# Cosine attention and FNet block on one core: new step priorities, other filler matmuls, and batch 1's scaling on two engines

## The chip, the cores and the metric

The kernel runs on one core of a Trainium2 chip. The metric is the device time of one launch in microseconds, as the median of three runs. The engines are TensorE (PE, matmuls), VectorE (DVE), ScalarE (ACT), GpSimd (POOL) and SyncE (SP, which here only issues DMAs). Each engine runs its own instructions in the order in which they were written; they meet through semaphores.

## The reference

```python
# q, k, v: (8, 12, 448, 64); w_ch1: (768, 3072); w_ch2: (3072, 768)
q_n = q / (np.linalg.norm(q, axis=-1, keepdims=True) + 1e-06)
k_n = k / (np.linalg.norm(k, axis=-1, keepdims=True) + 1e-06)
scores = np.matmul(q_n, k_n.transpose(0, 1, 3, 2)) / tau
attn = softmax(scores)
x = np.matmul(attn, v)            # heads side by side: (8, 448, 768)
u = x + np.real(np.fft.fft(np.fft.fft(x, axis=1), axis=2))
un = (u - mean(u)) / np.sqrt(var(u) + 1e-06)
out = u + np.maximum(un @ w_ch1, 0.0) @ w_ch2
```

## The kernel before

Eight batches go through four stages each: the norms and scaling of Q and K, attention, the two-dimensional Fourier mix, and a feed-forward block (FFN) with its layer norm. The stages of neighbouring batches overlap: while the FFN of batch b fills TensorE, the norms and the attention of batch b+1 run beside it.

**The order is planned when the kernel is built.** `Plan.add` (line 109) takes each step with the engines that may run it, an estimated length for each of them, a priority (`prio`, smaller goes first), the names that it reads and writes and, for a DMA, a time that the transfer takes on the queues (`serve`). `Plan.schedule` (line 153) then places step after step on the engine on which it can start earliest, breaking ties by priority; ScalarE and VectorE may wait a little for a more urgent step. A DMA is taken to land `DMA_LAT` (2.0 us) after its issue plus its `serve` time, shared with the other queue (lines 268 to 273). The result is one fixed list for each engine; `Plan.emit` (line 307) writes it out, with a semaphore wait for each dependency. At run time nothing is reordered: a step that waits holds everything behind it on its engine.

**Priorities** are 10 + 100 x batch for the norms, 13 to 18 above that for attention, 30 for the Fourier mix, and 5000 for the matmuls of the FFN, so that attention goes ahead of them. `SHIFT` (line 29) adds a number to single steps by name: `"t40": {0: 278.9}` makes the step t40 less urgent by 278.9.

**GpSimd and VectorE.** `PIECE` (line 58) and `PORT` (line 59) describe to the planner that GpSimd's elementwise steps are cut into pieces, and that certain VectorE steps that fall into such a piece are held until its end.

**Norms.** Batches 0 and 1 go through `first_norm` (line 577): the loads of K, Q and the tails in two groups of six heads (line 620), squares on ScalarE (627), sums on VectorE (631), `norms` (566; lines 571 to 575: logarithm, exponential, a small addition, a reciprocal), then the scaling: for each group three K, three Q steps of 128x384 (line 657) and three tail steps of 128x128 (line 653), all on VectorE. TensorE transposes the scaled tiles by matmuls with an identity (steps tk, tq, tt; lines 681, 693 to 695 and 706), and ScalarE or VectorE copies them out of PSUM (672, 716). The loads of batch 1 are put into the place of W2's chunks 5 to 11, which are loaded over them afterwards (line 553, on GpSimd's DMA queue). Batches 2 to 7 go through `norm` (line 719): GpSimd scales in pieces of 128x256 (line 764) and a DMA on SP's queue transposes (line 770).

**Attention** (`attn`, line 775): scores by row-paired matmuls (843, 855, 856), exponentials on ScalarE (823), the product with V (874, 880), and the division on VectorE (898, 900). **Fourier mix** (`fold`, 908, and `fft`, 984): folds on VectorE, two matmul stages (962 or 967, and 1005), sums into U (1021, 1033). The layer norm (1062 to 1071) writes UN; for batches 1 to 7 a DMA on SP's queue transposes it into UNT (line 1092).

**FFN.** `up` (1122): six matmuls a hidden tile against W1 (line 1137), then a ReLU out of PSUM (1153). `prod` (1161): the second matmuls (1168). Batches 1 to 7 pair their row tiles and save one product of eight by the Strassen-Winograd sums: of the hidden tiles on VectorE (`comb`, line 1263), and once of W2 (`sums`, line 1308: steps t1k to t4k for k = 0 to 2; t1 and t2 go before t4 by their operands; VectorE at line 1324 or GpSimd in four pieces at line 1326).

**Fillers.** `Plan.fill` (line 284) goes through TensorE's planned list and puts filler matmuls, whose results nobody reads, into planned gaps if a PSUM bank is free then. One filler step is 11 matmuls of 62 columns, planned at 0.34 us, one for each 0.4 us of the gap. It waits for the VectorE step that is the last planned to have ended by then. The first call (line 1381) covers 7.5 us to the first matmul of the FFN and fills gaps over 0.3 us; the second (line 1382) covers the rest and fills gaps over 1.2 us.

Of the kernel before, what the change touches and what calls it, by code (L numbers as in the profile page):

```python
# [26 lines left out]
DMA_LAT = 2.0  # L27

SHIFT = {
# [28 lines left out]
PIECE = {r"sc\d_\d": 0.63, r"f[avm]\dp_\d": 0.54, r"t\d\d": 0.94}  # L58
# [39 lines left out]
class Plan:  # L98
# [54 lines left out]
    def schedule(self):  # L153
# [65 lines left out]
        while left:  # L219
# [48 lines left out]
            if op.dma is not None:  # L268
                if t > now:
                    flow["sp"], flow["pool"] = drain(now, t)  # L270
                    now = t
                flow[e].append([op, op.end + DMA_LAT, op.serve])
                drain(now, None)
                if e == "sp":
                    sync.append(op)
# [8 lines left out]
    def fill(self, t0, t1, after, make, least=0.3):  # L284

        live = {x: [] for x in (0, 1, 2, 4, 6)}
        for op in self.ops:
            for t in op.acquire or ():
                live[t.slot if t.pool == "M" else 2 + 2 * t.slot].append((op.start, max(u.end for u in t.users), t))
# [1148 lines left out]
```

## Time and profile before

| what | before |
|---|---|
| median of 3 runs (lowest, highest) | 595.78 us (595.0, 596.48) |
| profiled execution | 595.06 us |
| its span, first to last instruction | 593.2 us |
| granted TensorE clock, mean | 0.996 |
| TensorE busy | 573.8 us (97%) |
| VectorE busy | 424.1 us (71%) |
| ScalarE busy | 352.0 us (59%) |
| GpSimd busy | 234.1 us (39%) |
| fillers (line 1377), TensorE | 418 matmuls before the FFN, 121 behind |

The first line of the profile's second part cuts the span into 40 slices of 14.8 us and gives busy tenths (9 is 90% or more); the lines below it give the clock that TensorE was granted and the DMA engines' share:

```profile
PE   5899899999899999999999999999999999999997
DVE  6979788888788868876888678976776469512222
POOL 8844235659554255523360454413540210200302
PEclk9999899999999999999999999999999999999999
DMA  9999997954289249584494179543931010310101
```

A busy TensorE here is one that has a matmul in its pipeline, not one at its peak, and the ends of matmuls are modelled. The groups of the scaling and of the DMA transposes, as the profile lists them (line, engine, operation, what it writes and reads, shape, count, busy us and mean ns; for DMAs the size and the time from issue to landing):

```profile
L764 POOL TENSOR_TENSOR QH<-STG,SM 128x256 bf16<-128x256 f32 x126 | 80.9, 668 | 83.1 <-DVE SM L575 65.9
UNT<-F SPq DMA_TRANSPOSE x25, 2.8
QT<-QH SPq DMA_TRANSPOSE x24, 4.1
KT<-QH SPq DMA_TRANSPOSE x18, 2.9
```

### The profile page before, as it was taken

How to read it: one execution, taken by the hardware profiler on the slowest of the kernel's cores; microseconds unless marked ns; L12 is line 12 of the kernel's file. 1: busy time of each engine (PE TensorE's matmuls, PEld its weight loads, DVE VectorE, ACT ScalarE, POOL GpSimd, SP SyncE). 2: the span in 40 equal slices, each digit the busy share in tenths (PEclk: the TensorE clock that was granted, in tenths of full speed). 3: DMA queues.
4: the chain of work that ended last, by engine and by line, in shares of the span. 5: the costliest groups of instructions: out<-in, count | busy, mean ns of one | idle time of the engine just before them, and what ended most of it. 6: DMA issues, size and time to landing. Idle time of an engine off the chain costs nothing.

```text
span 593.2 us, 15707 instructions
## 1 busy us (share of the span) xinstructions
PE 573.8 (97%) x6477; PEld 446.8 (75%) x6477; DVE 424.1 (71%) x975; ACT 352.0 (59%) x674; POOL 234.1 (39%) x344
## 2 busy tenths in 40 slices
PE   5899899999899999999999999999999999999997
PEld 4679687687578688778778688678878788778684
DVE  6979788888788868876888678976776469512222
ACT  7895787347865886458657756368537644224140
POOL 8844235659554255523360454413540210200302
PEclk9999899999999999999999999999999999999999
DMA  9999997954289249584494179543931010310101
GB/s 215 128 218 218 173 183 141 164 131 102 64 155 144 27 126 128 121 143 101 75 169 85 41 161 112 137 82 81 139 83 30 15 54 1 94 38 5 53 1 55
DMA packets 187640, 62.17 MB, mean 105 GB/s; under 512 B 166704, under 2 KB 185392, under 8 KB 187568
## 3 DMA queue, kind: packets, MB, share of 16 engines
q1 hardware_dynamic: 129648, 38.35, 34.3%
q0 software_dynamic: 57920, 22.81, 30.5%
q8 instruction: 51, 0.84, 0.6%
q14 instruction: 21, 0.17, 0.1%
HBM read 51.90 MB, written 11.01 MB: 106 GB/s over the span
## 4 chain that ended last, share of the span: by engine, by line
PE 84%; POOL 6%; DMA 4%; DVE 3%; SPq 2%; issue 1%; ACT 1%; POOLq 0%; DVEq 0%; ACTq 0%
PE PS L1137 34%; PE PS L1168 33%; PE PS L880 5%; PE PS L843 5%; DMA W2b<-in_k_dram 3%; SPq L620 2%; PE PS L967 2%; PE PS L874 2%; PE PS L1005 2%; POOL TX L1326 1%; DMA W1b<-in_moe_w_ch_dram 1%; PE PS L855 1%; POOL W1b L552 1%; POOL U L478 1%; PE PS L856 1%
## 5 line engine op out<-in xcount | busy, mean ns | idle before, releaser
L1137 PE MATMUL PS<-UNT,W1b 128*128 128x256 bf16 (+1 forms) x2304 | 236.3, 260 | 0.5 <-DVE HQ L1153 0.3
L1137 PEld LDWEIGHTS PS<-UNT,W1b 128*128 128x128 bf16 x2304 | 198.7, 98 | 25.4 <-issue 3.7
L823 ACT ACTIVATE E<-PS 128x900 bf16<-128x900 f32 x192 | 147.8, 827 | 31.8 <-PE PS L843 30.4
L1168 PE MATMUL PS<-W2b,HQ 128*128 128x384 bf16 x768 | 133.5, 326 | 0.0
L1153 ACT ACTIVATE HQ<-PS 128x512 bf16<-128x512 f32 x117 | 69.8, 598 | 87.7 <-PE PS L1137 86.7
L764 POOL TENSOR_TENSOR QH<-STG,SM 128x256 bf16<-128x256 f32 x126 | 80.9, 668 | 83.1 <-DVE SM L575 65.9
L1168 PEld LDWEIGHTS PS<-W2b,HQ 128*128 128x128 bf16 x768 | 73.5, 98 | 45.7 <-issue 1.7
L1263 DVE TENSOR_TENSOR HQ<-HQ 128x512 bf16<-128x512 bf16 x141 | 67.9, 502 | 44.2 <-ACT HQ L1153 31.1
L1193 POOL TENSOR_TENSOR OUTB<-OUTB,U 128x192 f32<-128x192 f32 x66 | 38.8, 608 | 139.2 <-ACT OUTB L1188 138.6
L1168 PE MATMUL PS<-TX,HQ 128*128 128x384 bf16 x396 | 69.9, 326 | 0.0
L1168 PEld LDWEIGHTS PS<-TX,HQ 128*128 128x128 bf16 x396 | 38.2, 98 | 24.2 <-issue 0.7
L880 PE MATMUL PS<-VB,E 128*128 128x65 bf16 x1152 | 51.1, 193 | 0.0
L757 DVE TENSOR_REDUCE SM<-QH 128x6 f32<-128x384 f32 x84 | 44.2, 536 | 8.5 <-ACT QH L755 8.2
L880 PEld LDWEIGHTS PS<-VB,E 128*128 128x128 bf16 x1152 | 47.6, 97 | 1.2
L1153 DVE TENSOR_SCALAR HQ<-PS 128x512 bf16<-128x512 f32 x45 | 31.1, 690 | 23.4 <-PE PS L1137 22.3
L755 ACT ACTIVATE QH<-STG 128x384 f32<-128x384 f32 x84 | 42.7, 521 | 6.2 <-DVE SM L757 6.0
L1222 POOL DMA_INDIRECT out_dram<-OUTB,IDX x20 | 20.8, 1039 | 63.9 <-DVE OUTB L1200 50.0
L843 PE MATMUL PS<-QT,KT 64*128 64x225 bf16 x576 | 39.9, 260 | 2.6 <-DVE X L900 2.3
L874 PE MATMUL PS<-VZ,E 128*128 128x130 bf16 x192 | 41.6, 219 | 0.5 <-ACT E L823 0.4
L1033 DVE TENSOR_TENSOR U<-ACG,X 128x384 bf16<-128x384 f32 (+3 forms) x70 | 39.8, 590 | 0.8
L1188 ACT ACTIVATE OUTB<-PS 128x384 f32<-128x384 f32 x33 | 16.2, 491 | 37.0 <-PE PS L1168 36.9
L843 PEld LDWEIGHTS PS<-QT,KT 64*128 64x128 bf16 x576 | 22.6, 94 | 16.3 <-issue 4.9
(134 smaller groups left out, 659.7 us busy)
## 6 DMA issues: line engine op xcount, KB each, us to landing
STG<-in_q_dram SPq DMA_DIRECT2D x18, 384.0 KB, 3.9
STG<-in_k_dram SPq DMA_DIRECT2D x18, 384.0 KB, 3.8
VB<-in_v_dram POOLq DMA_DIRECT2D x24, 192.0 KB, 6.9
W1b<-in_moe_w_ch_dram POOLq DMA_DIRECT2D x12, 384.0 KB, 6.4
W2b<-in_moe_w_ch_dram POOLq DMA_DIRECT2D x12, 384.0 KB, 6.9
out_dram<-OUTB SPq DMA_DIRECT2D x7, 384.0 KB
TX<-in_q_dram SPq DMA_DIRECT2D x2, 576.0 KB, 6.3
TX<-in_k_dram SPq DMA_DIRECT2D x2, 576.0 KB, 6.6
```

Of the source, the lines that this page charges most:

```text
L755: P.add("act", lambda a, sq=sq, src=buf[:, w * x:w * x + w]: a.activation(sq, src, ACTF.Square), t_act(w), pr, f"sq{i}_{b}", reads=bn, wri ...
L757: P.add("dve", lambda v, o=SS[:, i, H // ns * x:H // ns * (x + 1)], sq=sq: v.tensor_reduce(o, sq.rearrange("p (h d) -> p h d", d=DH), AX.X ...
L764: r = v.tensor_tensor(v3(qh)[:, h:h + 4], v3(buf)[:, h:h + 4], RN[:, i, h:h + 4].unsqueeze(2).to_broadcast((128, 4, DH)), AluOp.mult)
L823: return a.activation(o, self.PS[:, bk:bk + nc_, 0:SQ2], ACTF.Exp, scale=1.0 / self.tau)
L843: i = pe.matmul(self.PS[:, bk + h, c0:c0 + NK], self.KT[r, jj, kt * 128:(kt + 1) * 128], self.QT[r, jj, cols], start=True, stop=True)
L874: r = pe.matmul(o, st(6), self.VZ[:, j, :], start=not split, stop=(split and i == 0), skip_group_check=True)
L880: r = pe.matmul(o[:, 65 * h:65 * h + 65], st(2 * kt + h), self.VB[:, kt, 2 * j + h, :], start=(split and i == h == kt == 0), stop=((not sp ...
L1033: return v.tensor_tensor(U[o0:o0 + n, ut, cs].rearrange("p (i e) -> p i e", e=2), src, X[i0:i0 + n, x, cs].rearrange("p (i e) -> p i e", e ...
L1137: r = pe.matmul(self.PS[:, bk, x * n:(x + 1) * n], self.W1b[:, j, ft * 128:(ft + 1) * 128], self.UNT[:, j, cs], start=(j == 0), stop=(j == ...
L1153: return e.activation(o, i, ACTF.Relu) if e is self.nc.scalar else e.tensor_relu(o, i)
L1168: r = pe.matmul(self.PS[:, bk, 0:n], lhs(f), rhs(f), start=(start and f == 0), stop=(stop and f == NF // 2 - 1), skip_group_check=True)
L1263: P.add("dve", lambda v: v.tensor_tensor(cs(o), cs(a), cs(bq), op), 0.46, -0.5, f"{nm}{k}_{b}", reads=rd, writes=hr(o)(k))
```

## The change

Five things are changed, and the rest of the kernel is as before.

1. The scaling steps of batch 1 may go to VectorE or GpSimd, whichever the planner finds; GpSimd is planned at 0.98 us for K and Q and 0.42 us for a tail, as one piece each. Batch 0 stays on VectorE.
2. The planner takes a DMA transpose to land 0.4 us (`TR_LAT`) instead of 2.0 us after its issue, plus 1.3 us of `serve`, where it had 1.75 us for Q and K and 1.0 us for the normalized tiles.
3. A filler step is 6 matmuls of 128 columns instead of 11 of 62.
4. Fillers go into planned gaps from 0.4 us. Behind the start of the FFN they do so only where TensorE's planned use in some window of 3.4 us around the gap is under 0.75; the transposes tk, tq and tt count half in it. The last 20 us of the plan get none.
5. The table `SHIFT` is new throughout, so that the order of steps on every engine, the issues of DMAs among them, can differ.

The diff, with most of the table left out:

```diff
--- before.py
+++ after.py
@@ -25,37 +25,38 @@
 SEM_LAT = 0.11
 PE_LAT = 0.2
 DMA_LAT = 2.0
+TR_LAT = 0.4
 
 SHIFT = {
-    "ktd0": {0: 17.1}, "ix0": {0: -3.7}, "ix3": {0: 215.9}, "vz1": {0: 14.4}, "pads": {0: 1.8}, "ld_q0_0": {0: -131.9}, "ln0": {1: 4.8},
...
-    "pv21_1": {0: 2.3}, "x3_1": {0: -177.5}, "f10_1": {0: 97.4}, "ex5_1": {0: -284.8}, "relu16_0": {0: 127.8}, "t40": {0: 278.9}, "t32": {0:
...
+    "ix1": {0: 80.5}, "ld_k0_0": {0: -4.9}, "ldt0": {0: 60.6}, "nrm0": {0: -132.9, 2: -29.4, 3: 2.5}, "sqT0_0": {0: 86.3}, "scT2_0": {0: -6.6},
...
+    48.9}, "sqQ0_1": {0: -78.5}, "ln1": {1: 1.2}, "scK0_1": {0: 171.1}, "scK2_1": {0: 36.4}, "ek1_1": {0: -432.7}, "tq1_1": {0: 14.3},
+    "ld_t1_1": {0: -353.2}, "sqK1_1": {0: -6.1}, "ssK1_1": {0: 257.7}, "sqQ1_1": {0: -56.6}, "sqT1_1": {0: -2.4}, "tq4_1": {0: -139.8}, "tq5_1":
...
+    "t10": {0: -141}, "t40": {0: 441.4}, "t42": {0: 425.9}, "pq0_1": {1: 139.9}, "u0_1": {1: -96.4}, "pq1_1": {0: -32.8}, "u1_1": {0: 0.3, 5:
...
 }
 
 
 
-PIECE = {r"sc\d_\d": 0.63, r"f[avm]\dp_\d": 0.54, r"t\d\d": 0.94}
+PIECE = {r"sc[KQ]\d_1": 0.98, r"scT\d_1": 0.42, r"sc\d_\d": 0.63, r"f[avm]\dp_\d": 0.54, r"t\d\d": 0.94}
 PORT = r"eps\d|f[a01]\d_\d|g\d_\d|u\d+_\d|un\d_\d|s\d\d_\d|t\d\d|sc[KQT]\d_\d"
 
 
@@ -269,7 +270,7 @@
                 if t > now:
                     flow["sp"], flow["pool"] = drain(now, t)
                     now = t
-                flow[e].append([op, op.end + DMA_LAT, op.serve])
+                flow[e].append([op, op.end + (TR_LAT if op.name[:2] == "tr" else DMA_LAT), op.serve])
                 drain(now, None)
                 if e == "sp":
                     sync.append(op)
@@ -281,20 +282,24 @@
                     put(n)
         return max(op.end for op in self.ops)
 
-    def fill(self, t0, t1, after, make, least=0.3):
+    def fill(self, t0, t1, after, make, share=2.0):
 
         live = {x: [] for x in (0, 1, 2, 4, 6)}
         for op in self.ops:
             for t in op.acquire or ():
                 live[t.slot if t.pool == "M" else 2 + 2 * t.slot].append((op.start, max(u.end for u in t.users), t))
+        win, work = 3.4, [(op.start, op.end, 0.5 if op.name[:2] in ("tk", "tq", "tt") else 1.0) for op in self.order["pe"]]
+
+        def use(a):
+            return sum(z * (min(y, a + win) - max(x, a)) for x, y, z in work if x < a + win and y > a) / win
         out, t = [], t0
         for op in self.order["pe"]:
-            if op.start > t0 and op.end <= t1 + 1.0 and op.start - t > least:
+            if op.start > t0 and op.end <= t1 + 1.0 and op.start - t >= 0.4 and (share > 1.0 or min(use(t - win + 0.4 * x) for x in range(10)) < share):
                 bank = [x for x in live if not any(a < op.start and b > t for a, b, _ in live[x])]
 
                 for x in range(int((op.start - t) / 0.4)) if bank else ():
                     at = t + 0.4 * x
-                    new = Op(("pe",), make(bank[0], 11), (0.34,), 0, "warm")
+                    new = Op(("pe",), make(bank[0]), (0.34,), 0, "warm")
                     new.eng, new.start, new.end = "pe", at, at + 0.34
                     new.deps.add(after)
                     new.deps.add([o for o in self.order["dve"] if o.end + PE_LAT <= at + 0.1][-1])
@@ -658,7 +663,7 @@
                                                buf[:, s_].rearrange("p (h t d) -> p t h d", t=3, h=2),
                                                RN[:, o + 6 * j:o + 6 * j + 6].rearrange("p (h t) -> p t h", t=3).unsqueeze(3)
                                                .to_broadcast((128, 3, 2, DH)), AluOp.mult)
-                    sc.append(P.add("dve", fn, t_dve(21 * n) if i < 2 else 0.3, pg[g] + 0.1 * j, f"sc{nm}{jj}_{b}", reads=names + [f"RN_{g}{i}"],
+                    sc.append(P.add(("dve", "pool") if b else "dve", fn, ((t_dve(21 * n), 0.98) if i < 2 else (0.3, 0.42)) if b else t_dve(21 * n) if i < 2 else 0.3, pg[g] + 0.1 * j, f"sc{nm}{jj}_{b}", reads=names + [f"RN_{g}{i}"],
                                     writes=qhn[g][i] if j == 0 else [qhn[g][i][-1] + f"_{j}"],
                                     after=[sc0[i]] if j else []))
                     if j == 0:
@@ -770,7 +775,7 @@
             self.trs.append(P.add("sp", lambda sy, sem, dst=dst, qh=qh: sy.dma_start_transpose(dst, qh).then_inc(sem, 16),
                                   1.45, pr, f"tr{i}_{b}", reads=[f"QH{r}"],
                                   writes=[f"{nm}_{g}" for g in range(NJ)] + ([f"QTd_{g}" for g in range(NJ)] if t == 3 else []),
-                                  dma=(nm, 16), serve=1.75))
+                                  dma=(nm, 16), serve=1.3))
 
     def attn(self, b):
         P = self.P
@@ -1091,7 +1096,7 @@
                 continue
             self.last_tru = P.add("sp", lambda sy, sem, col=col, nb_=nb_: sy.dma_start_transpose(
                 self.UNT[:, :, col:col + 128], self.UN[:, nb_, :]).then_inc(sem, 16),
-                1.45, lp, f"tru{ui}_{b}", reads=[f"UN{nb_}"], writes=[f"uT{slot}" + x for x in ("", "x", "y")], dma=(f"uT{slot}", 16), serve=1.0)
+                1.45, lp, f"tru{ui}_{b}", reads=[f"UN{nb_}"], writes=[f"uT{slot}" + x for x in ("", "x", "y")], dma=(f"uT{slot}", 16), serve=1.3)
 
     def utiles(self, b):
 
@@ -1371,15 +1376,15 @@
         first = min(op.start for op in self.P.ops if op.name == "h0_0")
 
         def warm(w):
-            def make(bank, n):
+            def make(bank):
                 def fn(pe):
-                    for _ in range(n):
-                        r = pe.matmul(self.PS[:, bank, 450:512], w, w[:, 0:62], start=True, stop=True)
+                    for _ in range(6):
+                        r = pe.matmul(self.PS[:, bank, 0:128], w, w, start=True, stop=True)
                     return r
                 return fn
             return make
         self.P.fill(7.5, first, self.id_op, warm(self.ID))
-        self.P.fill(first, self.est, self.id_op, warm(self.W1b[:, 0, 0:128]), 1.2)
+        self.P.fill(first, self.est - 20.0, self.id_op, warm(self.W1b[:, 0, 0:128]), 0.75)
         self.P.emit(self.nc, self.es)
         self.es.close()
 
```

42 rows, old and new, of the table SHIFT are left out of this document.

## The prediction

> **What bounds the kernel now.** I read the profile's chain of waits first, then the engines' busy time in stretches, then the timelines of the places where TensorE is not full.
>
> ```profile
> 62.27 1.16 ACT OUTB L627
> 109.05 14.30 PE PS L1168 x88
> 123.35 3.68 PE PS L1377 x121
> 127.03 3.94 PE PS L1137 x36
> ```
>
> These are pieces of the chain (start, length, what). From 69 us on it is nearly all TensorE. Even its fillers (L1377) stand on it: nothing else released the matmul at 127.03.
>
> ```profile
> 60.00:67.00 7.00, 5.10 (x47) 3.77 (x45) 4.94 (x15) 4.48 (x10) 1.24 (x3) 0.97 2.21 160
> 67.00:71.00 4.00, 3.98 (x32) 2.92 (x34) 2.58 (x5) 2.77 (x5) 1.27 (x2) 0.62 1.12 195
> 123.00:127.00 4.00, 4.00 (x126) 3.80 (x124) 3.36 (x9) 2.65 (x9) 3.55 (x4) 1.00 0.87 124
> 147.00:152.00 5.00, 2.72 (x37) 1.63 (x36) 4.97 (x8) 2.63 (x5) 4.63 (x6) 1.00 0.35 79
> 182.00:510.00 328.00, 328.00 (x3532) 255.35 (x3530) 252.28 (x599) 202.14 (x399) 114.57 (x172) 1.00 0.59 92
> ```
>
> ```profile
> 66.00:67.00 1.00, 0.85 (x10) 0.68 (x8) 0.67 (x3) 0.55 (x1) 0.13 (x1) 0.80 1.79 168
> 67.00:68.00 1.00, 0.98 (x9) 0.92 (x11) 1.00 (x2) 0.09 (x1) 0.56 (x1) 0.50 1.18 195
> 68.00:69.00 1.00, 1.00 (x12) 0.56 (x9) 0.78 (x1) 0.68 (x2) 0.00 (x0) 0.50 1.10 192
> 69.00:70.00 1.00, 1.00 (x7) 0.73 (x5) 0.71 (x2) 1.00 (x2) 0.23 (x1) 0.50 1.11 204
> ```
>
> Columns of both: stretch, its length, busy us of TensorE, its weight loads, VectorE, ScalarE and GpSimd, granted clock, DMA share, GB/s. From 182 to 510 TensorE is never idle and waits for nobody, so no order of steps gains there. What can be had lies before 182: thin TensorE from 60 to 67, a clock of 0.62 behind it, a stretch of fillers alone at 123, and a hole at 147.
>
> ```profile
> 121.96 1.23 SPq L1092 DMA_TRANSPOSE UNT<-F  x1
> 145.49 1.33 DVE L1324 TENSOR_TENSOR TX<-W2b,TX 128x1536 bf16<-128x1536 bf16 x1
> 147.88 2.97 DVE L1263 TENSOR_TENSOR HQ<-HQ 128x512 bf16<-128x512 bf16 x3
> 151.01 0.69 DVE L900 TENSOR_TENSOR X<-PS,RD 128x512 bf16<-128x512 f32 x1
> 146.18 4.39 POOL L1326 TENSOR_TENSOR W2b<-W2b 128x384 bf16<-128x384 bf16 x4 [0.17 <-POOL QH L764]
> 151.75 0.46 PE L843 MATMUL PS<-QT,KT 64*128 64x225 bf16 x6 [1.77 <-DVE X L900]
> ```
>
> Timelines: start, length. The sum is made against the profiled execution, 595.06 us (span 593.2 and 1.86 around it); the median of the runs, 595.78, lies 0.72 above, which I add at the end.
>
> **Fillers, their shape.** Eleven of 62 columns took 0.334 us (3.68 us for 121); six of 128 cost 6 x 56 = 0.335 us (L1137 with 128 columns: 36 in 2.01 us on the chain). Cost: nothing, and the narrow ones already held the clock at 1.00 from 123 to 127.
>
> **Fillers, their place.** From 62 to 67 us no filler ran; TensorE idled 1.02 us at 63 and in pieces after it. The rows of single microseconds then show a clock of 0.80, 0.50, 0.50, 0.50 from 66 to 70, and matmuls on the chain from 67.02 to 70.87. What they lose is 0.2 + 3 x 0.5 = 1.7 us. The new rule fills gaps from 0.4 us where use in 3.4 us is under 0.75, with transposes at half weight, and this place is thin by that measure. Ends: 1.7 gained; nothing, if the planned gaps are too short. I take **-1.7**: the stretch is the thinnest behind 60 us.
> The Trainium skill (TensorE: Matmul & The Clock Gate, Part 1) says that a window of about 3.4 us without activity halves the clock and that a busy one brings it back. The drop here, three rows and a bit, agrees in length; by that rule the sum is the same. Its Part 4 says that transposes in transpose mode don't count as activity; these are ordinary matmuls with the identity, so no run here shows it.
>
> **Transposes as measured.** For the normalized tiles (L1092) the planner has 1.45 + 2.0 + 1.0 = 4.45 us from issue to landing, after the change 1.45 + 0.4 + 1.3 = 3.15; the profile's median is 2.8. The one at 121.96 took 3.3 and landed at 125.26, yet fillers ran to 127.03: 1.77 us of planned work that was not needed. With 1.3 us less of planned wait, three fillers fewer: **-1.3** (ends: -1.7 and 0).
> For Q and K (L770) it goes from 5.2 to 3.15, against medians of 4.1 and 2.9 and 8.1 at worst. Cost at nothing: the last of batch 2 is issued at 134.2 and of batch 3 at 186.7, while their score matmuls (L843) start at 191.5 and 261.7. Without that cover a late one would cost 0.95 (4.1 - 3.15) for each of six batches, 5.7 us.
>
> **Scaling of batch 1.** Twelve K and Q scalings (L657, 0.55 us) and six of tails (L653, 0.30) may leave VectorE: 12 x 0.55 + 6 x 0.30 = 8.4 us. GpSimd's price by its nearest row, the scaling of later batches (L764, 668 ns for 256 columns): 1.00 us for 384 and 0.33 for 128. Each is 0.45 later but runs beside VectorE. Group 0 (60.86 to 66.56) is six and three, 4.2 us on VectorE. With k of the six on GpSimd the two finish together near k = 3 and GpSimd is the later from k = 5 on. The chain holds 1.25 us of them (64.46 to 65.71), so the ends are half of that gained, 0.6, and two in series on GpSimd lost, 0.9. I take 0. Queued behind a waiting scaling on GpSimd are the W2 loads (L553) and the V loads of batch 1 (L803); the last W2 load goes out at 90.42, lands 6.9 us later (median), and its last chunk is wanted at 100.75: 3.4 us of cover.
> The Trainium skill (GPSIMD Engine Reference, 1. Specifications) says that GpSimd shares SBUF access with VectorE and contends with its instructions of two SBUF inputs. The trace agrees: L1263 takes 0.99 us beside L1326, against a median of 0.43. It speaks against this part; what it does here is priced in the part on priorities and in the GpSimd rival.
>
> **Priorities.** The SHIFT table is new throughout. What can be placed: "t42" and "t40" sink (their priority numbers rise by 425.9 and 162.5). The sum at 145.49 is the last of three in a row (after its t1 and t2), so t42; it stands before the two L900 that TensorE waits for at 148.02 and 151.75 (0.52 + 1.77 = 2.29 us idle). Away from there it frees 1.33 us; as four pieces on GpSimd it may hold one more L1263 by 0.99 - 0.43 = 0.56. I take -1.33 + 0.56, about **-0.7**. Ends: -2.3 (whole hole gone) and +1.7 (three L1263 held). The DMAs that move: the loads of batch 1 on SP (L620) and W1/W2 on GpSimd's queue, in a stretch with a DMA share of 1.0 to 2.5, so what one gains another gives up; 0, with ends of 3.1 either way from the row at 62.27: ScalarE's square of K1 waited for its load until then, and the small norm step queued behind it ran only at 63.43 though its input was ready near 60.3.
>
> **Sum.** -1.7 - 1.3 + 0 - 0.7 = -3.7: 595.06 - 3.7 = 591.4 profiled, **592.1** as a median. Its own range: all gains whole, -1.7 - 1.7 - 2.3 = -5.7, to -1.7 alone: 590.1 to 594.1.
>
> **Rivals.**
> *The front goes too:* the norm step no longer sits behind K1's square. 3.1 more: 589.0. For: that stall is a queue order, which priorities can change. Against: "sqK1_1" rises rather than sinks.
> *A wash:* the thin stretch is filled, but TensorE then waits for the same tiles; the hole at 147 moves on. Only the 1.3 at 123 remains, and a new stall of that size eats it: 595.8.
> *GpSimd becomes the front's bound (slower):* place: group 0 and group 1 (60 to 82 us). All nine of a group on GpSimd take 6 x 1.00 + 3 x 0.33 = 7.0 instead of 4.2, 2.8 later, twice; it decides from five K/Q scalings of a group on. 5.6 - 1.7 - 1.3 = +2.6: 598.4. For: VectorE is 86% busy from 71 to 90 and GpSimd 37%, so an earliest-start planner sends work there. Against: the planner knows 0.98 for it.
> *Fillers hold TensorE (slower):* each filler waits for VectorE's latest planned step; before, that made TensorE idle 2.65 us once (L1377 behind L631). Two such in 60 to 182: 5.3 - 1.7 = +3.6: 599.4. For: many thin gaps there. Against: at 123 none waited.
> *No effect as said:* planned gaps under 0.4 us everywhere; counted with the wash.
>
> **How the numbers follow.** About 0.3% (1.8 us) can be told from no change, so faster is under 594.0 and slower over 597.6. Chances: forecast 0.41, front too 0.17, wash 0.13, GpSimd 0.17, fillers 0.12. Faster 0.58, same 0.13, slower 0.29. The range goes from 586.5 (front too with every gain whole, 589.0 - 1.6 - 0.4 = 587.0, and a little) to 599.5 (fillers).
>
> **What will show it.** Right: fillers between 60 and 70 with a clock of 1.00 there; at up(1)'s start eight or fewer fillers, or none past the landing; under 1 us idle at the second sums; L764-like scalings of batch 1 on GpSimd, two to four a group. Wrong: idle of TensorE released by GpSimd's scalings before 90 us, fillers with VectorE as releaser, or TensorE waiting after 182.

## The result and the profile after

| what | before | after |
|---|---|---|
| median of 22 runs each (lowest, highest) | 596.98 us (594.39, 600.15) | 599.76 us (596.14, 604.44) |
| profiled execution, its span | 595.06, 593.2 us | 598.87, 597.0 us |
| TensorE busy | 573.8 us | 573.7 us |
| GpSimd busy | 234.1 us | 246.0 us |

The ratio is 1.0051 with a 95% interval of 1.0032 to 1.007: the change makes the kernel slower by 0.5%, some 3.0 us. Line numbers behind the changed parts are 5 higher than before: L843 is now L848, L1137 is L1142, L1326 is L1331. The fillers are L1377 before and L1382 after; edits of the experiments move them further, to L1402 at most.

Stretches after, with the columns of the prediction's table:

```profile
60.00:67.00 7.00, 5.75 (x70) 4.86 (x68) 5.17 (x12) 4.44 (x11) 3.95 (x7) 1.00 2.06 171
67.00:71.00 4.00, 3.73 (x47) 2.84 (x45) 3.42 (x5) 3.17 (x7) 1.06 (x2) 1.00 0.88 153
123.00:127.00 4.00, 4.00 (x40) 2.84 (x39) 3.79 (x9) 1.54 (x4) 0.89 (x2) 1.00 0.69 118
147.00:152.00 5.00, 2.24 (x16) 1.18 (x15) 2.47 (x3) 1.94 (x4) 4.69 (x7) 0.83 0.54 118
182.00:510.00 328.00, 327.32 (x3541) 255.94 (x3539) 245.85 (x583) 206.24 (x404) 117.93 (x177) 1.00 0.62 94
```

The clock at 67 to 71 is 1.00 where it was 0.62: the fillers do there what they were to do. The stretch of fillers at 123 is shorter. But the hole at 147 to 152, where TensorE had idled, has not closed, it is emptier than before (2.24 us busy for 2.72) and has a clock of 0.83. From 182 to 510 TensorE is busy for 327.32 of 328 us, where it was for all 328.

TensorE's timeline after, at the start of the second batch's FFN and at its scores (in brackets the idle time before a row and what ended it):

```profile
125.85 1.84 PE L1382 MATMUL PS<-W1b 128*128 128x128 bf16 x30
127.53 13.27 PE L1142 MATMUL PS<-UNT,W1b 128*128 128x256 bf16 x120
141.93 0.56 PE L848 MATMUL PS<-QT,KT 64*128 64x225 bf16 x8 [1.12 <-issue]
...
145.05 2.11 PE L1173 MATMUL PS<-W2b,HQ 128*128 128x384 bf16 x12
149.93 0.58 PE L848 MATMUL PS<-QT,KT 64*128 64x225 bf16 x8 [2.76 <-DMA KT<-QH]
...
150.79 3.58 PE L1173 MATMUL PS<-W2b,HQ 128*128 128x384 bf16 x12
```

These L848 are the score matmuls of **batch 2**, and each waits for a DMA transpose (the first row's releaser reads "issue"; the Q transpose had gone out at 139.10 and lands 2.8 us later). The two idle pieces make 3.9 us. The twelve matmuls at 150.79 take 3.58 us where twelve of the same shape at 145.05 take 2.11: half clock (granted 0.50) behind the idle piece, 1.5 us more.

The chain of waits after says why the transposes are late:

```profile
131.66 3.82 POOL TX L1331 x4
135.64 3.44 POOL QH L769 x3
139.24 3.79 POOL TX L1331 x4
143.26 1.18 issue
144.45 2.62 POOL QH L769 x2
147.08 2.80 DMA KT<-QH
```

On GpSimd stand, one behind the other: the sum t40 of W2 (L1331), the scaling of batch 2's last Q rows (L769), the sum t21, and the scaling of its last K rows. The K transpose goes out at 147.08. Before, t40 ran on VectorE (0.95 us), both scalings stood ahead of GpSimd's next two sums, and that transpose went out at 134.21. These are the rows of the kernel before, from its timelines of VectorE, GpSimd, SP's queue and TensorE:

```profile
130.15 0.95 DVE L1324 TENSOR_TENSOR TX<-W2b,TX 128x1536 bf16<-128x1536 bf16 x1
129.10 2.47 POOL L764 TENSOR_TENSOR QH<-STG,SM 128x256 bf16<-128x256 f32 x3 [0.18 <-ACT HQ L1153]
131.74 2.44 POOL L764 TENSOR_TENSOR QH<-STG,SM 128x256 bf16<-128x256 f32 x3 [0.17 <-ACT HQ L1153]
134.35 8.28 POOL L1326 TENSOR_TENSOR TX<-W2b,TX 128x384 bf16<-128x384 bf16 x8 [0.17 <-POOL QH L764]
131.60 1.78 SPq L770 DMA_TRANSPOSE QT<-QH  x1
134.21 1.48 SPq L770 DMA_TRANSPOSE KT<-QH  x1
136.14 0.56 PE L843 MATMUL PS<-QT,KT 64*128 64x225 bf16 x8
139.36 0.56 PE L843 MATMUL PS<-QT,KT 64*128 64x225 bf16 x8
```

The two transposes landed 2.9 and 3.8 us after their issue, at 134.5 and 138.0. The two score steps stand at 136.14 and 139.36, so each had some 1.5 us to spare.

How far TensorE had come, after minus before: each of its matmuls but the fillers is valued at the time from one start to the next at full clock, and those begun by a moment are added up. The difference is -2.6 us at 102, 0.0 at 126, -0.6 at 138, -3.6 at 156, and -3.1 to -4.9 from there on. So a loss of 2.6 us ahead of 102 is gone at 126, as the kernel before runs nothing but fillers from 123 to 127 (below, the hole at 123), and the loss that stays arises between 138 and 156.

### The profile page after: what moved, and what is told of

The parts are those of the page before. It is cut to its first block, busy times and chain, and to the rows that moved or that the text cites. A ratio compares the mean times of both kernels' runs of the same rounds, so it can differ in the third digit from the quotient of the medians.

```text
span 597.0 us, 15197 instructions
## 1 busy us (share of the span) xinstructions
PE 573.7 (96%) x6214; PEld 446.8 (75%) x6214; DVE 418.6 (70%) x961; ACT 352.9 (59%) x675; POOL 246.0 (41%) x360
## 4 chain that ended last, share of the span: by engine, by line
PE 81%; DMA 6%; DVE 4%; POOL 4%; ACT 3%; issue 1%; SPq 0%; POOLq 0%; DVEq 0%; ACTq 0%
PE PS L1173 32%; PE PS L1142 31%; PE PS L885 5%; PE PS L848 5%; DMA W2b<-in_moe_w_ch_dram 3%; DMA STG<-in_k_dram 2%; PE PS L972 2%; PE PS L1010 2%; PE PS L879 2%; POOL TX L1331 1%; ACT E L828 1%; PE PS L1382 1%; POOL QH L769 1%; DVE U L1038 1%; PE PS L860 1%
## 5 line engine op out<-in xcount | busy, mean ns | idle before, releaser
L1142 PE MATMUL PS<-UNT,W1b 128*128 128x256 bf16 (+1 forms) x2304 | 235.0, 259 | 0.7 <-ACT HQ L1158 0.7
L1142 PEld LDWEIGHTS PS<-UNT,W1b 128*128 128x128 bf16 x2304 | 198.2, 98 | 24.9 <-issue 4.1
L828 ACT ACTIVATE E<-PS 128x900 bf16<-128x900 f32 (+1 forms) x192 | 147.5, 830 | 31.9 <-PE PS L848 29.7
L769 POOL TENSOR_TENSOR QH<-STG,SM 128x256 bf16<-128x256 f32 x126 | 82.5, 680 | 89.3 <-DVE SM L580 56.0
L1268 DVE TENSOR_TENSOR HQ<-HQ 128x512 bf16<-128x512 bf16 x141 | 68.0, 501 | 39.3 <-ACT HQ L1158 22.7
L848 PE MATMUL PS<-QT,KT 64*128 64x225 bf16 x576 | 39.6, 259 | 6.8 <-DMA KT<-QH 2.8
L1205 DVE TENSOR_TENSOR OUTB<-PS,OUTB 128x384 f32<-128x384 f32 x33 | 18.3, 553 | 30.7 <-PE PS L1173 28.6
```

Source lines behind the costliest of these rows:

```text
L769: r = v.tensor_tensor(v3(qh)[:, h:h + 4], v3(buf)[:, h:h + 4], RN[:, i, h:h + 4].unsqueeze(2).to_broadcast((128, 4, DH)), AluOp.mult)
L828: return a.activation(o, self.PS[:, bk:bk + nc_, 0:SQ2], ACTF.Exp, scale=1.0 / self.tau)
L848: i = pe.matmul(self.PS[:, bk + h, c0:c0 + NK], self.KT[r, jj, kt * 128:(kt + 1) * 128], self.QT[r, jj, cols], start=True, stop=True)
L1142: r = pe.matmul(self.PS[:, bk, x * n:(x + 1) * n], self.W1b[:, j, ft * 128:(ft + 1) * 128], self.UNT[:, j, cs], start=(j == 0), stop=(j == ...
L1268: P.add("dve", lambda v: v.tensor_tensor(cs(o), cs(a), cs(bq), op), 0.46, -0.5, f"{nm}{k}_{b}", reads=rd, writes=hr(o)(k))
```

## The experiments

The runs but those with other fillers edit the finished order of one of the two kernels, not the priorities: a planner run with other priorities would move everything at once. A helper moves one step to an engine, in front of another step:

```python
        def move(name, eng, at):
            order = self.P.order
            op = next(o for v in order.values() for o in v if o.name == name)
            order[op.eng].remove(op)
            op.eng = eng
            i = next(i for i, o in enumerate(order[eng]) if o.name == at)
            order[eng].insert(i, op)
```

### The sums of W2 ahead of the scalings

Both sums behind the scalings on GpSimd, in the changed kernel:

```diff
+        move('t40', 'pool', 't32')
+        move('t21', 'pool', 't32')
```

> The changed kernel with two steps moved on GpSimd: the W2 sums t40 and t21 go behind the last K scaling of batch 2 (sc6_2) instead of before it; every other step keeps engine and order, TensorE's list and the shorter planned landing of transposes included. Theory A (the sums on GpSimd hold back the scaling, and so the transpose that TensorE waits for): the waits of 1.12 us at 141 and 2.76 us at 147 vanish, and with them the half clock from 150 to 153 (1.5 us); the sums end about 1.3 us later on VectorE, so 3 to 5 us less than the changed kernel, that is about 595.5. Theory B (TensorE's list asks for the transposed tiles 2 us too early, because the landing was planned shorter): a wait of about 2 us stays at the second score step of batch 2, and the time falls by 2 us at most.

Measured: 596.57 us, ratio to before 1.0023 (1.0004 to 1.0042). The waits for the transposes are gone, but only about 1.7 us came back, where theory A had 3 to 5. t40 now ends at 139.1, the other sums are chained to it by the names that they write, and VectorE waits 5.3 us for GpSimd in front of its next sum. A reduction of batch 3's norms queues behind that sum, ScalarE's logarithm waits 3.93 us for the reduction, a ReLU queues behind the logarithm, and TensorE waits 2.54 us for the ReLU. The late scaling was exchanged for a late sum: the waits went as in theory A, the size is theory B's.

t40 on VectorE, where the kernel before had it, and t21 behind the scalings:

```diff
+        move('t40', 'dve', 't11')
+        move('t21', 'pool', 't32')
```

> The changed kernel with the sum t40 put back on VectorE in front of t11, where the kernel before has it, and t21 on GpSimd behind the last K scaling of batch 2. Theory A: the same waits vanish, and the chain of sums is not held by GpSimd, so 4 to 5.4 us less than the changed kernel, about 595. Theory B: as for the run with both on GpSimd, 2 us at most.

Measured: 594.35 us, ratio **0.9969** (0.9952 to 0.9986), by the ratios 4.9 us less than the changed kernel, and faster than the kernel before. Its TensorE timeline at the same place:

```profile
128.00 13.26 PE L1142 MATMUL PS<-UNT,W1b 128*128 128x256 bf16 x120
141.20 0.56 PE L848 MATMUL PS<-QT,KT 64*128 64x225 bf16 x8
141.69 2.79 PE L1142 MATMUL PS<-UNT,W1b 128*128 128x256 bf16 x24
144.32 2.11 PE L1173 MATMUL PS<-W2b,HQ 128*128 128x384 bf16 x12
146.37 0.56 PE L848 MATMUL PS<-QT,KT 64*128 64x225 bf16 x8
```

No row has an idle piece before it, and none follows up to 160. By the count of TensorE's work this kernel stands at -1.0 us against before at 138 and at +1.6 at 156, the changed kernel at -0.6 and -3.6. Between the two moments that is 5.6 us, near the 3.9 of waits and the 1.5 of half clock. The half clock belongs to that one profiled execution. Over all executions the mean granted clock is 0.9958 in the changed kernel and 0.9979 in this one, which makes 1.3 us of 597. No run moves t21 alone, so its share of the 4.9 is not shown. This run leaves t42 on GpSimd, where the change had put it, and the 2.3 us that TensorE idled at 147 to 152 in the kernel before are gone in its trace; the part of the prediction that t42 stood for looks right, though no run moves that step alone.

The converse, in the kernel before: only t40, from VectorE to GpSimd in front of the scaling of the last Q rows.

```diff
+        move('t40', 'pool', 'sc5_2')
```

> The kernel before with one edit to the finished order: the sum step t40 goes from VectorE to GpSimd, in front of the scaling of batch 2's last Q rows. Theory A (the new priorities cost what they cost because this one step of some 3.8 us stands on GpSimd before batch 2's last two scalings): the last K transpose is issued near 138 instead of 134.2 and lands near 142, so the second score step of batch 2, at 139.4 before, waits some 2.4 us; slower by 2.4 to 3.8 us, ratio 1.004 to 1.0065, with a wait of TensorE for KT<-QH in the trace. Theory B (the step is harmless there, and it is the whole of the new order that costs): ratio 0.999 to 1.002 and no such wait.

Measured: 599.54 us, ratio 1.0046 (1.0022 to 1.0069), 2.7 us slower. GpSimd's and TensorE's rows, from the two timelines of this run:

```profile
132.26 3.51 POOL L1326 TENSOR_TENSOR TX<-W2b,TX 128x384 bf16<-128x384 bf16 x4
135.94 3.43 POOL L764 TENSOR_TENSOR QH<-STG,SM 128x256 bf16<-128x256 f32 x3 [0.17 <-POOL TX L1326]
```

```profile
130.12 9.33 PE L1137 MATMUL PS<-UNT,W1b 128*128 128x256 bf16 x84
142.37 0.56 PE L843 MATMUL PS<-QT,KT 64*128 64x225 bf16 x8 [2.91 <-DMA QT<-QH]
```

One step of 3.5 us on another engine's list costs 2.9 us of TensorE idle, in the range of theory A. It was the Q transpose that was missed, the first of the two, not the K transpose. The sizes fit: the step's 3.5 us, and 0.96 more for the scaling behind it (3.43 us for 2.47), less the 1.6 us that the Q transpose had to spare (landed at 134.5, wanted at 136.14).

### The fillers

The new filler steps and their rule alone, in the kernel before:

```diff
-    def fill(self, t0, t1, after, make, least=0.3):
+    def fill(self, t0, t1, after, make, share=2.0):
...
-        self.P.fill(first, self.est, self.id_op, warm(self.W1b[:, 0, 0:128]), 1.2)
+        self.P.fill(first, self.est - 20.0, self.id_op, warm(self.W1b[:, 0, 0:128]), 0.75)
```

> The kernel before with the new filler rule alone (six matmuls of 128 columns, gaps from 0.4 us where use is thin); all other steps keep engine and order. The rule adds one filler step, near 63 us, and keeps the eleven at 123 us. If the half clock from 66.8 to 70 us was a cost of its own, as the prediction took it: clock 1.00 there and 1.7 us less than the kernel before. Rival: TensorE waits there for tiles in any case, or one filler is too little for the clock: within 0.5 us of the kernel before.

Measured: 593.83 us, ratio 0.9967 (0.994 to 0.9993), 2.0 us faster, with an interval that only just clears 1. The mean granted clock over its executions is 0.9976 against 0.9956, which makes 1.2 of the 2.0 us. In its profiled execution TensorE idles 1.70 us at 65.8 and the clock stays at 1.00:

```profile
67.00:71.00 4.00, 2.71 (x32) 2.25 (x34) 3.72 (x11) 2.80 (x6) 0.52 (x1) 1.00 1.24 162
```

This execution took 596.33 us, 2.5 more than the run's median, so it shows the clock and not the gain. The one filler step that the rule adds here ran at 67.86, behind the idle piece; that this step held the clock is not shown.

The opposite, the changed kernel with the old fillers:

```diff
-        self.P.fill(first, self.est - 20.0, self.id_op, warm(self.W1b[:, 0, 0:128]), 0.75)
+        self.P.fill(first, self.est, self.id_op, warm(self.W1b[:, 0, 0:128]), 1.2)
```

> The changed kernel with the old fillers (62 columns wide, placed as before), the rest of it unchanged. Theory A (the fillers' place is worth the same 2 us in both kernels, as the run with the new fillers alone gave 0.9967 on the kernel before): ratio 1.0075 to 1.009, granted clock at 66 to 71 us well under 1. Theory B (in the new order TensorE idles less there, so the fillers' place is worth nothing): ratio 1.004 to 1.006.

Measured: 599.33 us, ratio 1.0049 (1.0025 to 1.0073), the same as with the new ones, as theory B had it. The clock does fall, to 0.81 over 60 to 67 in its profiled execution. TensorE stands 1.4 us further back at 66 than with the new fillers. Half of that comes back, as it then waits less: from 90 to 123 it is busy for the full 33.00 us (31.83 in the changed kernel). At 102 it is 0.8 behind, at 138 it is 0.7 behind, and at 156 it is 1.0 ahead. Its two waits for the transposes are as long as in the changed kernel (1.37 and 2.49 us), but behind the second one the clock stays at 1.00. So in these two executions a front loss of 0.7 is hidden by a clock that happened to hold later. Why the 2 us of the fillers do not show in the changed kernel's times stays open.

### The landing at 123

The kernel before without the last five of its eleven filler steps at 123:

```diff
+        pe = self.P.order["pe"]
+        late = [o for o in pe if o.name == "warm" and o.start > 100]
+        for o in late[-5:]:
+            pe.remove(o)
```

> The kernel before without the last five of the eleven filler steps at 123 us. Theory A (the landing step of the prediction: the fillers outlast the landing by 1.77 us, and all of it comes through): first matmul of up(1) near 125.3, ratio 0.997 (1.8 us faster). Theory B (later waits take it back, the wait for the K transposes near 139 or for the normalised X near 147): up(1) starts near 125.3 all the same, but the waits near 139 to 152 grow by what was gained, ratio 0.9995 to 1.001.

Measured: 596.95 us, ratio 0.9995 (0.9976 to 1.0014). Theory B. TensorE's timeline:

```profile
126.54 2.03 PE L1377 MATMUL PS<-W1b 128*128 128x62 bf16 x66
128.51 2.79 PE L1137 MATMUL PS<-UNT,W1b 128*128 128x256 bf16 x24
132.37 6.72 PE L1137 MATMUL PS<-UNT,W1b 128*128 128x256 bf16 x60 [1.07 <-ACT HQ L1153]
...
142.80 0.56 PE L843 MATMUL PS<-QT,KT 64*128 64x225 bf16 x8 [0.49 <-DMA KT<-QH]
```

The run with t40 on GpSimd in the kernel before keeps the five and had an equally late front in its profiled execution. It came to its fillers at 126.45 and to up(1) at 130.12, with 9.33 us of matmuls in one piece. Here up(1) starts 1.6 us earlier, waits 1.07 for a ReLU that stands behind two squares of batch 3 on ScalarE, and 0.49 for the K transpose: 1.56 given back. The fillers behind the landing had filled time that the next two waits would have taken.

In both runs the fillers start some 3 us later than in the kernel before (123.35 in the prediction's chain). That is scatter between executions, and the traces show where it is from in these. ScalarE's square of K1 waits 2.00 us for its load in the kernel before and starts at 62.27, the row of the prediction's chain. In this run:

```profile
65.80 1.16 ACT L627 ACTIVATE OUTB<-W2b 128x1152 f32<-128x1152 f32 x1 [4.70 <-DMA W2b<-in_k_dram]
```

One load lands 3.5 us later in one execution than in another; a ReLU queued behind its square holds TensorE 3.72 us, and the clock is 0.50 from 66 to 72.

### The front

The second half of batch 1's GpSimd scalings on VectorE, in the changed kernel:

```diff
+        move('scK3_1', 'dve', 'scK5_1')
+        move('scK4_1', 'dve', 'scK5_1')
+        move('scT3_1', 'dve', 'rd0_1')
+        move('scT4_1', 'dve', 'x0_1')
+        move('scQ5_1', 'dve', 'eq4_1')
+        move('scT5_1', 'dve', 'eq4_1')
```

> The changed kernel with the six scalings of batch 1's second group that the plan gave to GpSimd (K3, K4, Q5 and three tails) put back on VectorE at their place in the order; the first group stays on GpSimd. Theory C (the scaling is stuck on GpSimd's queue behind W2 load issues that wait for earlier loads, and TensorE loses 3.3 us between 72 and 102 us by that): TensorE's wait of 1.08 us at 75 and the 0.45 us at 79 vanish and 1.5 to 3 us of the time. Rival: these waits are small, and what TensorE lost there comes from ScalarE's squares of batch 2 that wait for their loads: under 1 us.

Measured: 599.59 us, ratio 1.0049 (1.0033 to 1.0065): no change from 1.0051, as the rival had it. At 84 TensorE stands 0.9 us better than in the changed kernel, at 96 both stand at some -2.5 against before: it waits more for exponentials (1.07 and 1.40 us for 0.72 and 1.17). These stand on ScalarE behind squares of batch 2, which wait 1.55 and 2.15 us for loads that go out at 79.3 (the staging loads; before: 75.2). Those loads are gated by the W2 piece W2_7, which the new priorities put sixth behind batch 1's V loads on GpSimd's list instead of fourth. So W2_7 in front of W2_3, fourth, with t40 left on GpSimd and with t40 on VectorE:

```diff
+        move('W2_7', 'pool', 'W2_3')
```

> The changed kernel with the load order alone edited, t40 left on GpSimd. Theory A (front loss and the late scalings are two separate losses that add): ratio near 1.0013, 2.2 us less than the changed kernel's 1.0051. Theory B (the front is absorbed, at 123 or in the wait for the K transpose at 147): ratio 1.004 to 1.006.

> The changed kernel with t40 back on VectorE (as in the earlier run) and one more edit: the load of the W2 piece that gates batch 2's staging loads is issued in front of the two other W2 loads of its group, fourth instead of sixth. Theory A (the front's loss of about 3 us comes from that order and reaches the end through the landing of the second normalised rows, 127.5 instead of 125.3): staging loads near 75 instead of 80, up(1) near 125.5 instead of 128.2, ratio 0.992 to 0.9945 (2 us less than with t40 alone, 0.9969). Theory B (the hole at 123 absorbs the front whatever its length): ratio 0.996 to 0.998.

Measured: 604.68 us, ratio 1.0121 (1.0093 to 1.015), and 599.69 us, ratio 1.0047 (1.0033 to 1.0062): each over 4 us slower than without the edit (1.0051 and 0.9969). Neither theory had that. GpSimd's timeline of the second:

```profile
73.94 2.19 POOL L558 DMA_DIRECT2D W2b<-in_moe_w_ch_dram  x3 [4.75 <-DMA W2b<-in_moe_w_ch_dram]
80.63 0.70 POOL L558 DMA_DIRECT2D W2b<-in_moe_w_ch_dram  x1 [4.50 <-DMA W2b<-in_moe_w_ch_dram]
81.35 1.76 POOL L662 TENSOR_TENSOR QH<-W2b,SM 128x384 bf16<-128x384 f32 x2
```

The issues wait for earlier pieces to land (each for the third one before it in number), and everything on GpSimd waits with them: the scalings of K3 and K4 start at 81.35 instead of 75.61. This is the prediction's rival of GpSimd as the front's bound, near its full size: TensorE waits 4.8 us in one piece for GpSimd's scaling. The cause is not the rival's, which had the scalings too long and the loads queued behind them; here the scalings queue behind a load. It also shows that a front loss is taken up only to a point. By the count of work the run with t40 on VectorE stood 7.9 us behind the kernel before at 114 and 5.0 at 126, and the same kernel without the load edit 3.1 and 0.3: the hole at 123 took up some 2.8 us in each. Measured, the load edit costs 4.7 us (0.0078 of 597).

t40 and the six scalings on VectorE together:

> The changed kernel with t40 back on VectorE and the second half of batch 1's GpSimd scalings (K3, K4, Q5 and their tails) on VectorE too. Theory A (the front's loss comes from batch 2's late staging loads, not from the scalings, as the scalings alone moved gave nothing): ratio 0.995 to 0.998, as t40 alone, 0.9969. Theory B (now that the later wait is gone, the scalings' 1 us shows): ratio 0.993 to 0.9955.

Measured: 595.16 us, ratio 0.9965 (0.9947 to 0.9982), as with t40 alone and as theory A had it. And the same with W2_4 and W2_7 at their old places, now that no K or Q scaling of the second half stands behind them on GpSimd:

```diff
+        move('W2_4', 'pool', 'W2_0')
+        move('W2_7', 'pool', 'W2_3')
```

> The run before this one and the load order of the kernel before for the two W2 pieces that matter: W2_4 as the first, W2_7 right behind the first tails. Nothing of batch 1's scaling stands behind a waiting load issue on GpSimd then but three tails. Theory A (the front's loss is the place of W2_7 plus in-order GpSimd, and it reaches the end): staging loads of batch 2 near 75, first matmul of up(1) near 126 instead of 128, ratio 0.991 to 0.9945. Theory B (the loads are bound by the memory traffic of the front and land when they land, whatever the order): staging loads at 78 to 80, ratio 0.995 to 0.998.

Measured: **594.1 us, ratio 0.9943** (0.9922 to 0.9965), the lowest ratio of the study, from six executions. The staging loads go out at 75.73, as theory A said, but up(1) starts at 128.62 and not near 126: now the first three K scalings stood behind a waiting W2 issue, and TensorE waited 3.5 us for them. With those three in front of the W2 issues:

```diff
+        move('scK0_1', 'pool', 'W2_4')
+        move('scK1_1', 'pool', 'W2_4')
+        move('scK2_1', 'pool', 'W2_4')
```

> The run with t40, the second group's scalings and the load order, and batch 1's first three K scalings put in front of the W2 issues on GpSimd (there they began at 62.5 behind an issue that had waited 1.3 us, and TensorE waited 3.5 us for them). Theory A (GpSimd takes its queue in order, so a scaling behind a waiting issue is late by the wait and the issues, and this loss reaches the end): TensorE's wait for the K scalings 1 to 2 us, ratio 0.990 to 0.993. Theory B (the loads are now the later by the scalings' 2.7 us, and batch 2's staging loads with them, near 78): ratio 0.994 to 0.997.

Measured: 594.0 us, ratio 0.9954 (0.9931 to 0.9978), in theory B's range but not by its mechanism. In its profiled execution that wait is gone and the staging loads still go out at 75.40, so TensorE ends the first FFN's main stretch at 124.96 instead of 127.1; and then it idles for VectorE:

```profile
117.81 7.15 PE L1173 MATMUL PS<-W2b,HQ 128*128 128x384 bf16 x43
127.41 3.38 PE L1402 MATMUL PS<-W1b 128*128 128x128 bf16 x30 [2.45 <-DVE U L1038]
```

The fillers themselves (here L1402) wait for a step of VectorE, a small sum into U, and up(1) starts behind them at 130.58. This execution took 596.42 us, 2.4 above the run's median; whether the faster ones idle there too is not shown. The intervals of this run, of the two before it and of t40 alone overlap; which of them is the best is open, and so is how much of the front could be had if VectorE's rows at 120 to 127 were earlier.

## Why the prediction was wrong

**The sum of the parts.** Forecast 592.1, measured 599.76, 0.26 above the range. Measured part by part against before: the fillers alone -2.0 us; all of the change with t40 back on VectorE (and t21 behind the scalings) -1.8; t40 and t21 where the planner put them, 4.9 on top (0.9969 to 1.0051). What makes up the -1.8 is not shown run by run. In the trace of that run up(1) starts 1.1 us later than before (128.00 for 126.87), and the hole of 2.3 us at 147 to 152 is gone.

**The step that failed** is the one on priorities: "'t42' and 't40' sink", priced at "about -0.7" with ends of -2.3 and +1.7. I asked what place they leave, and of the list that they enter only how GpSimd would slow VectorE there. Who stands behind them on GpSimd I did not ask. t40 left VectorE, where it took 0.95 us, for GpSimd, where it takes 3.8, and there it stands in front of scalings that a transpose, and then TensorE, waits for. The price of +0.56 for "one more L1263" on VectorE named the wrong victim. The measured one is 2.7 us for t40 alone in the kernel before, and 4.9 for t40 and t21 in the changed one, with the half clock in it. Some of this is that GpSimd's steps got longer: the planner has 1.85 us for a scaling of three pieces, and the two took 3.43 and 3.87 in the changed kernel, 1.86 and 1.84 in the run with both sums behind them. No run separates that from the place of the sums.

**The step that hid it** is the cover of the Q and K transposes: "their score matmuls (L843) start at 191.5 and 261.7", so "cost at nothing". These rows belong to the batch after the one meant. The score matmuls of batch 2 are the L843 rows from 136 us on. Its last K transpose, issued at 134.21, landed at 138.0, and its second score step ran at 139.36: the cover was 1.4 us, not 57. With that row read rightly, a step of over 1.4 us in front of those scalings was to be feared.

**Transposes as measured, -1.3.** The mechanism was right: the fillers that outlasted the landing are gone. The size was not: taking them away by themselves gave 0.9995, since a ReLU and the K transpose take the 1.6 us back in the trace. I had not asked what is late next behind this gain.

**Fillers' place, -1.7:** the time came out near it in the kernel before (-2.0); nothing shows in the changed kernel. The parts are not additive.

**Scaling of batch 1, 0:** moving six of the twelve back changes nothing, so that much of the 0 held; the other six were not moved back. The price of a tail on GpSimd, 0.33 us, was too low: three took 1.80. Of the rival one sign came: ahead of 90 us TensorE waited for GpSimd's scalings in five pieces, 3.0 us in all. But the hole at 123 takes up a front loss of that size, though not the 4.7 us that the load order put on top. The rival's 598.4 is near the measured time by another cause, scalings of batch 2 at 131 to 147, not of batch 1 at 60 to 82.

**Fillers hold TensorE:** not in the changed kernel behind 60 us; once, 2.45 us, in the last run.

**The signs.** Three signs of being right came although the time was wrong: filler steps between 60 and 70 with a clock of 1.00, five of them at up(1)'s start and none past the landing, and three K and Q scalings a group on GpSimd. None of these looks at the place where the time was lost. The fourth, under 1 us idle at the second sums, failed with 2.76 us there.

## What to carry to other kernels

Price a moved step on the list that it enters: who stands behind it there, how much slack those have, and what it costs on that engine (here four times as much). Read slack between a producer and its consumer of the same batch, and check the batch by the count of such rows; one wrong row turned 1.4 us into 57. A gain ahead of a hole, or a loss, is worth only what the next wait leaves of it, so measure the parts on both kernels before adding them.

## What the runs showed of the hardware

**GpSimd and VectorE slow each other.** One piece of GpSimd's scaling (128x256) takes a median of 0.61 us over the kernel before (the mean is 0.67); three take 1.86 us at 132.37 in the run with t40 on VectorE and 3.87 at 143.19 in the changed kernel, beside three sums of W2 on VectorE. In the run with t40 on VectorE four sum pieces took 4.84 us on GpSimd and VectorE's six L1268 5.53 us, 0.92 each:

```profile
144.66 4.84 POOL L1331 TENSOR_TENSOR W2b<-W2b 128x384 bf16<-128x384 bf16 x4 [2.22 <-DVE TX L1329]
```

```profile
145.63 5.53 DVE L1268 TENSOR_TENSOR HQ<-HQ 128x512 bf16<-128x512 bf16 x6
```

Alone, an L1268 takes 0.41 us. The Trainium skill (GPSIMD Engine Reference, 1. Specifications) says that GpSimd's access to SBUF is shared with VectorE and contends with VectorE instructions of two SBUF inputs; these rows agree, with a factor of 2.1 for the scaling and 2.2 for L1268. The sums' pieces went from 0.88 us (3.51 for four in the run with t40 on GpSimd in the kernel before) to 1.21.

**The length of an idle piece does not settle the clock.** In the changed kernel TensorE idles 2.76 us to 149.93, and single microseconds behind it show:

```profile
150.00:151.00 1.00, 1.00 (x11) 0.66 (x12) 0.00 (x0) 0.45 (x1) 1.00 (x2) 0.67 0.97 222
151.00:152.00 1.00, 1.00 (x4) 0.44 (x3) 0.00 (x0) 1.00 (x3) 0.86 (x3) 0.50 0.66 149
152.00:153.00 1.00, 1.00 (x4) 0.44 (x3) 0.43 (x1) 1.00 (x2) 0.83 (x2) 0.50 0.00 0
```

With t40 moved alone in the kernel before it idles 2.91 us to 142.37, and the clock from 142 to 146 is 1.00. The changed kernel with the old fillers idles 2.49 us to 150.63, at the same step, and the clock there is 1.00 too. In the prediction's rows the clock was 0.50 behind a thin stretch whose longest idle piece was 1.02 us. So something other than the length of the piece matters, what lies around it or when it falls; no run here separates the two. Of the 4.9 us the 1.5 of half clock are a part that another execution may not have.
